# Chunked retention attention and channel mix: scores on 64-row tiles, decay moved to key and eviction, a 128x128 state for two heads, mix in blocks of 256 tokens one block behind, everything in written order

## The chip, the core and the metric

The kernel runs on one core of one Trainium2 chip. The metric is the device time of the whole program in microseconds (us). Times are medians of several executions. The traces come from one profiled execution each, whose span is some 1 to 3 us shorter than the median.

In these kernels TensorE (PE) runs the matmuls and transposes, and PEld is its weight load; VectorE (DVE) and ScalarE (ACT) run elementwise operations, those that empty TensorE's accumulators (PSUM) among them; GpSimd (POOL) runs elementwise operations between tiles in SBUF and issues the casting loads, and SyncE (SP) issues plain loads and stores. The page of the kernel before counts 1456, 1456, 214, 178 and 19 instructions on PE, PEld, DVE, ACT and POOL.

## The reference, cut to what matters

```python
# q, k, v: [B=4, H=8, S=768, D=64] float32
gamma = 1 - 2 ** (-5 - arange(H)); scale = 1 / sqrt(D)
for t in range(S):
    state = gamma * state + einsum("bhd,bhe->bhde", k[:, :, t], v[:, :, t])
    y[:, :, t] = scale * einsum("bhd,bhde->bhe", q[:, :, t], state)
x = y as [B, S, 512]
x_prev = x shifted by one token, zero first
xk = mu_k * x + (1 - mu_k) * x_prev          # token mix, for the keys
xr = mu_r * x + (1 - mu_r) * x_prev          # token mix, for the gate
out = sigmoid(xr @ w_r) * (maximum(xk @ w_k, 0) ** 2 @ w_v)   # 512 -> 1024 -> 512
```

The recurrence is worked in chunks of 128 tokens: masked scores inside a chunk, and a state of 64x64 per head carried from chunk to chunk. There are 24 chunks.

## The kernel before

The kernel before lets a scheduler interleave the attention of one batch with the mix of the batch before. These are the parts that matter. The decay is multiplied into q and k on DVE, in one operation of 1024 columns per chunk. The mix works in halves of 384 tokens, and its difference `dx` is made on POOL.

```python
# attention, per chunk (cut)
nc.vector.tensor_tensor(out=qks, in0=qk32, in1=Gqk, op=ALU.mult)       # L199: decay on q and k
... transposes of q and k by TensorE, copied out by ACT (zero-padded qptz) and DVE (kpt)
nc.tensor.matmul(pA[:, jj], lhsT=kpt[:, j, :], rhs=qptz[:, :, j, :])   # L214: 128 rows, half of them zeros
nc.vector.tensor_tensor(out=a2t[...], in0=pA, in1=causal8[...])        # L218
...
nc.scalar.copy(out=xT[:, :, col : col + C], in_=pY)                    # L238: attention output
nc.vector.tensor_tensor(out=s16g, in0=pS, in1=ghv2, op=ALU.mult)       # L256: state, 256 columns

# mix, per half of 384 tokens (cut)
nc.gpsimd.tensor_tensor(out=dx, in0=xcur, in1=xprev, op=ALU.subtract)  # L129
for fo in range(NJ):
    nc.vector.scalar_tensor_tensor(out=xk16[:, fo], in0=dx[:, fo], scalar=muk4[...], in1=xprev[:, fo], ...)  # L135
    nc.vector.scalar_tensor_tensor(out=xr16[:, fo], ...)               # L139
... keys (L148), relu and square (ACT), values (L160), gate (L166), product osb (DVE), store
```

Of the kernel before, what the change touches and what calls it, by code (L numbers as in the profile page):

```python
# [9 lines left out]
F16 = mybir.dt.float16  # L11
# [4 lines left out]
KSC = 64.0  # L16
DX_ON_POOL = True
KPT_ON_ACT = True


def _f16(x):
    return np.asarray(x, dtype=np.float32).astype(np.float16)
# [3 lines left out]
def kernel(  # L26
# [20 lines left out]
    TM = 384  # L47
    NTM = S // TM
    COLS = S + 1
    NCO = dm // P  # L50
    NFO = dff // P
    ntb = TM // P
    INV_KSC2 = 1.0 / (KSC * KSC)
# [3 lines left out]
    e3 = np.ones((1, 1, D))  # L57
    Gqk_np = np.stack(
        [(0.125 * gam[None, :, None] ** ar[:, None, None]) * e3,
         (gam[None, :, None] ** (-ar[:, None, None])) * e3], axis=1,  # L60
    )
    causal_np = (ar[None, :] >= ar[:, None]).astype(np.float64)
    causal8_np = np.broadcast_to(causal_np[:, None, :], (C, H, C)).copy()
    hp_of_p = np.arange(P) // 64
    h_pj = 2 * np.arange(NJ)[None, :] + hp_of_p[:, None]
    ghv2_np = np.broadcast_to((gam[h_pj] ** C)[:, :, None], (P, NJ, D)).copy()
    eye = np.eye(D)
    dz = np.zeros((P, 2, D))
    dz[0:64, 0] = eye
    dz[64:128, 1] = eye  # L70
    ident_np = np.eye(P)

    const_pool = ctx.enter_context(tc.tile_pool(name="consts", bufs=1))
    wpool = ctx.enter_context(tc.tile_pool(name="weights", bufs=1))
    xpool = ctx.enter_context(tc.tile_pool(name="xstage", bufs=1))
    qk_pool = ctx.enter_context(tc.tile_pool(name="qkp", bufs=3))
    v_pool = ctx.enter_context(tc.tile_pool(name="vp", bufs=2))
    awork = ctx.enter_context(tc.tile_pool(name="awork", bufs=3))
    spool = ctx.enter_context(tc.tile_pool(name="spool", bufs=3))
    mwork = ctx.enter_context(tc.tile_pool(name="mwork", bufs=2))  # L80
    psT = ctx.enter_context(tc.tile_pool(name="psT", bufs=1, space=bass.MemoryType.PSUM))
    psA = ctx.enter_context(tc.tile_pool(name="psA", bufs=1, space=bass.MemoryType.PSUM))
    psY = ctx.enter_context(tc.tile_pool(name="psY", bufs=1, space=bass.MemoryType.PSUM))
    psS = ctx.enter_context(tc.tile_pool(name="psS", bufs=1, space=bass.MemoryType.PSUM))
    psZ = ctx.enter_context(tc.tile_pool(name="psZ", bufs=1, space=bass.MemoryType.PSUM))
    psV = ctx.enter_context(tc.tile_pool(name="psV", bufs=2, space=bass.MemoryType.PSUM))
    psR = ctx.enter_context(tc.tile_pool(name="psR", bufs=1, space=bass.MemoryType.PSUM))

    c32_np = np.concatenate([Gqk_np.reshape(P, -1), ghv2_np.reshape(P, -1)], axis=1)
    c16_np = np.concatenate([ident_np.reshape(P, -1), causal8_np.reshape(P, -1)], axis=1)  # L90
    c32d = nc.inline_tensor(c32_np.astype(np.float32), name="c32")
    c16d = nc.inline_tensor(c16_np.astype(np.float16), name="c16")
    c32 = const_pool.tile(list(c32_np.shape), F32, name="c32_sb")
    c16 = const_pool.tile(list(c16_np.shape), F16, name="c16_sb")
    nc.sync.dma_start(out=c32, in_=c32d.ap())
    nc.sync.dma_start(out=c16, in_=c16d.ap())
    n0 = Gqk_np.reshape(P, -1).shape[1]
    Gqk = c32[:, 0:n0].rearrange("p (a h d) -> p a h d", a=2, h=H)
    ghv2 = c32[:, n0:].rearrange("p (j e) -> p j e", j=NJ)
    ident = c16[:, 0:P]  # L100
    causal8 = c16[:, P : P + H * C].rearrange("p (h t) -> p h t", h=H)

    xT = xpool.tile([P, NJ, B * COLS], F32, name="xT")
    for b in range(B):
        nc.vector.memset(xT[:, :, b * COLS : b * COLS + 1], 0.0)

    qptz0 = xpool.tile([P, 2, NJ, C], F16, name="qptz0")
    qptz1 = xpool.tile([P, 2, NJ, C], F16, name="qptz1")
    qptzb = [qptz0, qptz1]
    nc.vector.memset(qptz0, 0.0)  # L110
    nc.vector.memset(qptz1, 0.0)

    muk4 = const_pool.tile([P, NCO], F32, name="muk4")
    mur4 = const_pool.tile([P, NCO], F32, name="mur4")
    nc.sync.dma_start(out=muk4, in_=moe_mu_k.rearrange("(co ci) -> ci co", ci=P))
    nc.sync.dma_start(out=mur4, in_=moe_mu_r.rearrange("(co ci) -> ci co", ci=P))

    wk16 = wpool.tile([P, NCO, dff], F16, name="wk16")
    wv16 = wpool.tile([P, NFO, dm], F16, name="wv16")
    wr16 = wpool.tile([P, NCO, dm], F16, name="wr16")  # L120

    def moe_block(b):
        for half in range(NTM):
            colx = b * COLS + 1 + half * TM
            xcur = xT[:, :, colx : colx + TM]
            xprev = xT[:, :, colx - 1 : colx + TM - 1]
            dx = mwork.tile([P, NJ, TM], F32, tag="dx")
            if DX_ON_POOL:
                nc.gpsimd.tensor_tensor(out=dx, in0=xcur, in1=xprev, op=ALU.subtract)  # L129
            else:  # L130
                nc.vector.tensor_tensor(out=dx, in0=xcur, in1=xprev, op=ALU.subtract)
            xk16 = mwork.tile([P, NJ, TM], F16, tag="xk16")
            xr16 = mwork.tile([P, NJ, TM], F16, tag="xr16")
            for fo in range(NJ):
                nc.vector.scalar_tensor_tensor(  # L135
                    out=xk16[:, fo], in0=dx[:, fo], scalar=muk4[:, fo : fo + 1],
                    in1=xprev[:, fo], op0=ALU.mult, op1=ALU.add,
                )
                nc.vector.scalar_tensor_tensor(  # L139
                    out=xr16[:, fo], in0=dx[:, fo], scalar=mur4[:, fo : fo + 1],  # L140
                    in1=xprev[:, fo], op0=ALU.mult, op1=ALU.add,
                )
            krel = mwork.tile([P, NFO, TM], F32, tag="krel")
            k2 = mwork.tile([P, NFO, TM], F16, tag="k2")
            for fo8 in range(NFO):
                pZ = psZ.tile([P, TM], F32, tag="pZ")
                for co in range(NCO):
                    nc.tensor.matmul(  # L148
                        pZ, lhsT=wk16[:, co, fo8 * P : fo8 * P + P], rhs=xk16[:, co, :],
                        start=(co == 0), stop=(co == NCO - 1),  # L150
                    )
                nc.scalar.activation(out=krel[:, fo8, :], in_=pZ, func=AF.Relu, scale=KSC)  # L152
                if fo8 % 4 == 3:
                    hsl = slice(fo8 - 3, fo8 + 1)
                    nc.scalar.activation(out=k2[:, hsl], in_=krel[:, hsl], func=AF.Square)  # L155
            for tb in range(ntb):
                tsl = slice(tb * P, tb * P + P)
                pV = psV.tile([P, dm], F32, tag="pV")
                for fo8 in range(NFO):
                    nc.tensor.matmul(  # L160
                        pV, lhsT=k2[:, fo8, tsl], rhs=wv16[:, fo8, :],
                        start=(fo8 == 0), stop=(fo8 == NFO - 1),
                    )
                pR = psR.tile([P, dm], F32, tag="pR")
                for co in range(NCO):
                    nc.tensor.matmul(  # L166
                        pR, lhsT=xr16[:, co, tsl], rhs=wr16[:, co, :],
                        start=(co == 0), stop=(co == NCO - 1),
                    )
                rsb = mwork.tile([P, dm], F32, tag="rsb")  # L170
                nc.scalar.activation(out=rsb, in_=pR, func=AF.Sigmoid)  # L171
                osb = mwork.tile([P, dm], F32, tag="osb")
                nc.vector.scalar_tensor_tensor(  # L173
                    out=osb, in0=pV, scalar=INV_KSC2, in1=rsb, op0=ALU.mult, op1=ALU.mult,
                )
                s0 = half * TM + tb * P
                nc.sync.dma_start(out=out[b, s0 : s0 + P, :], in_=osb)

    for b in range(B):
        v16 = v_pool.tile([P, H, NCH, D], F16, tag="v16")  # L180
        nc.gpsimd.dma_start(
            out=v16.rearrange("t h c d -> t (h c) d"),
            in_=v[b].rearrange("h (c t) d -> t (h c) d", t=C),
        )
        if b == 0:
            nc.gpsimd.dma_start(out=wk16, in_=moe_w_k.rearrange("(co ci) f -> ci co f", ci=P))
            nc.gpsimd.dma_start(out=wv16, in_=moe_w_v.rearrange("(fo fi) e -> fi fo e", fi=P))
            nc.gpsimd.dma_start(out=wr16, in_=moe_w_r.rearrange("(co ci) e -> ci co e", ci=P))
# [100 lines left out]
```

## Time and profile before

| what | before |
|---|---|
| median of 3 runs, profiled span | 268.99 us, 266.6 us |
| busy PE, DVE, ACT, POOL | 193.7, 147.1, 110.0, 33.7 us |
| first mix matmul starts at | 55.8 us |
| columns that TensorE streams, all / by 56 us | 357,376 / 22,656 |
| time at half clock in the clock records | 44.1 us |

Half clock means that a clock record of the profile gives 0.50 as the granted share of TensorE's full clock. Read the busy time of PE as how long some matmul was in flight, not as a limit that was reached: at the full clock 357,376 columns take some 149 us (an estimate, from matmuls of 512 columns that start 216 ns apart in the trace of before, some 2.4 columns a ns).

### The profile page before, as it was taken

How to read it: one execution, taken by the hardware profiler on the slowest of the kernel's cores; microseconds unless marked ns; L12 is line 12 of the kernel's file. 1: busy time of each engine (PE TensorE's matmuls, PEld its weight loads, DVE VectorE, ACT ScalarE, POOL GpSimd, SP SyncE). 2: the span in 40 equal slices, each digit the busy share in tenths (PEclk: the TensorE clock that was granted, in tenths of full speed). 3: DMA queues.
4: the chain of work that ended last, by engine and by line, in shares of the span. 5: the costliest groups of instructions: out<-in, count | busy, mean ns of one | idle time of the engine just before them, and what ended most of it. 6: DMA issues, size and time to landing. Idle time of an engine off the chain costs nothing. (4 is left out here: it accounts for less than half of the span.)

```text
span 266.6 us, 3608 instructions
## 1 busy us (share of the span) xinstructions
PE 193.7 (73%) x1456; PEld 107.2 (40%) x1456; DVE 147.1 (55%) x214; ACT 110.0 (41%) x178; POOL 33.7 (13%) x19
## 2 busy tenths in 40 slices
PE   0020356683999997683999994859999987598883
PEld 0010234461454555451544553634554464233431
DVE  1022146889955256989644179799451479912103
ACT  1010122233375753431564662244747653255640
POOL 8200000407000001215000004040000040400000
PEclk9999999978699998786899997597999999889999
DMA  5999999736954426509907045300320110000203
GB/s 152 170 185 197 189 157 191 162 81 41 211 126 135 122 57 185 115 2 102 173 0 199 1 140 138 80 2 0 79 100 20 48 73 0 0 4 31 87 0 118
DMA packets 81472, 25.82 MB, mean 97 GB/s; under 512 B 76080, under 2 KB 77616, under 8 KB 81456
## 3 DMA queue, kind: packets, MB, share of 16 engines
q1 hardware_dynamic: 54720, 19.83, 31.3%
q0 software_dynamic: 26736, 5.77, 23.8%
q8 instruction: 11, 0.18, 0.3%
q14 instruction: 5, 0.04, 0.0%
HBM read 25.07 MB, written 6.29 MB: 118 GB/s over the span
## 5 line engine op out<-in xcount | busy, mean ns | idle before, releaser
L148 PE MATMUL pZ<-xk,wk 128*128 128x384 f16 x256 | 59.2, 347 | 1.9 <-ACT krel L152 1.1
L199 DVE TENSOR_TENSOR qks<-qk,c_sb 128x1024 f16<-128x1024 f32 x24 | 34.9, 1468 | 45.3 <-DMA qk<-in_k_dram 26.3
L160 PE MATMUL pV<-wv,k 128*128 128x512 f16 x192 | 48.0, 380 | 3.5 <-ACT k L155 3.3
L152 ACT ACTIVATE krel<-pZ 128x384 f32<-128x384 f32 x64 | 31.2, 488 | 44.7 <-PE pZ L148 44.6
L218 DVE TENSOR_TENSOR a2t<-pA,c_sb 128x512 f16<-128x512 f32 x48 | 33.0, 688 | 27.6 <-PE pA L214 27.3
L166 PE MATMUL pR<-wr,xr 128*128 128x512 f16 x96 | 33.3, 425 | 15.6 <-DVE xr L139 14.8
L129 POOL TENSOR_TENSOR dx<-xT 128x1536 f32<-128x1536 f32 x8 | 22.0, 2749 | 175.0 <-ACT xT L238 156.3
L148 PEld LDWEIGHTS <-wk 128*128 128x128 f16 x256 | 26.2, 103 | 28.4 <-issue 14.0
L173 DVE SCALAR_TENSOR_TENSOR osb<-pV,rsb 128x512 f32<-128x512 f32 x24 | 16.4, 686 | 31.8 <-PE pV L160 13.7
L238 ACT COPY xT<-pY 128x512 f32<-128x512 f32 x24 | 14.1, 586 | 47.1 <-PE pY L233 39.7
L139 DVE SCALAR_TENSOR_TENSOR xr<-dx,mur,xT 128x384 f16<-128x384 f32 x32 | 33.4, 1044 | 0.0
L228 PE MATMUL pY<-a2t,v 128*64 128x128 f16 x192 | 25.7, 251 | 9.6 <-DVE a2t L218 9.0
L206 ACT COPY qptz<-pT 64x512 f16<-64x512 f16 x24 | 13.8, 576 | 35.4 <-PE pT L203 35.4
L202 PE MATMUL pT<-c_sb,qks 128*128 128x128 f16 x96 | 17.6, 251 | 14.3 <-DVE qks L199 14.3
L160 PEld LDWEIGHTS <-k 128*128 128x128 f16 x192 | 17.3, 98 | 23.5 <-ACT k L155 6.1
L243 PE MATMUL pS<-v,qks 128*64 128x64 f16 x192 | 9.5, 218 | 22.3 <-DVE qks L199 19.8
L155 ACT ACTIVATE k<-krel 128x1536 f16<-128x1536 f32 x16 | 23.7, 1484 | 0.5
L214 PE MATMUL pA<-qptz,kpt 128*128 128x256 f16 x96 | 22.2, 318 | 1.8 <-DVE a2t L218 1.8
L171 ACT ACTIVATE rsb<-pR 128x512 f32<-128x512 f32 x24 | 14.3, 595 | 21.5 <-PE pR L166 13.7
L233 PE MATMUL pY<-qptz,s16g 128*64 128x128 f16 x160 | 22.2, 247 | 0.0
L228 PEld LDWEIGHTS <-v 128*64 128x64 f16 x192 | 17.3, 122 | 12.2 <-issue 11.5
L166 PEld LDWEIGHTS <-xr 128*128 128x128 f16 x96 | 10.0, 104 | 28.4 <-DVE xr L139 19.6
(25 smaller groups left out, 152.0 us busy)
## 6 DMA issues: line engine op xcount, KB each, us to landing
qk<-in_q_dram SPq DMA_DIRECT2D x24, 256.0 KB, 3.8
qk<-in_k_dram SPq DMA_DIRECT2D x24, 256.0 KB, 4.1
out_dram<-osb SPq DMA_DIRECT2D x24, 256.0 KB, 2.1
v<-in_v_dram POOLq DMA_DIRECT2D x4, 768.0 KB, 12.8
wk<-in_moe_w_k_dram POOLq DMA_DIRECT2D x1, 1024.0 KB, 19.9
wv<-in_moe_w_v_dram POOLq DMA_DIRECT2D x1, 1024.0 KB, 25.8
c_sb<-c SPq DMA_DIRECT2D x1, 640.0 KB, 3.6
wr<-in_moe_w_r_dram POOLq DMA_DIRECT2D x1, 512.0 KB, 28.4
```

What stands on the lines that cost most here:

```text
L129: nc.gpsimd.tensor_tensor(out=dx, in0=xcur, in1=xprev, op=ALU.subtract)
L139: nc.vector.scalar_tensor_tensor(out=xr16[:, fo], in0=dx[:, fo], scalar=mur4[:, fo : fo + 1], in1=xprev[:, fo], op0=ALU.mult, op1=ALU.add,)
L148: nc.tensor.matmul(pZ, lhsT=wk16[:, co, fo8 * P : fo8 * P + P], rhs=xk16[:, co, :], start=(co == 0), stop=(co == NCO - 1),)
L152: nc.scalar.activation(out=krel[:, fo8, :], in_=pZ, func=AF.Relu, scale=KSC)
L155: nc.scalar.activation(out=k2[:, hsl], in_=krel[:, hsl], func=AF.Square)
L160: nc.tensor.matmul(pV, lhsT=k2[:, fo8, tsl], rhs=wv16[:, fo8, :], start=(fo8 == 0), stop=(fo8 == NFO - 1),)
L166: nc.tensor.matmul(pR, lhsT=xr16[:, co, tsl], rhs=wr16[:, co, :], start=(co == 0), stop=(co == NCO - 1),)
L199: nc.vector.tensor_tensor(out=qks, in0=qk32, in1=Gqk, op=ALU.mult)
L214: nc.tensor.matmul(pA[:, jj], lhsT=kpt[:, j, :], rhs=qptz[:, :, j, :], start=(jj == 0), stop=(jj == 1),)
L218: nc.vector.tensor_tensor(out=a2t[:, 4 * tt : 4 * tt + 4, :], in0=pA, in1=causal8[:, 0:4, :], op=ALU.mult,)
L228: nc.tensor.matmul(o, lhsT=v16[:, h, c, :], rhs=a2t[:, h, :], start=first, stop=(last and c == 0), skip_group_check=(hp == 1),)
L233: nc.tensor.matmul(o, lhsT=s16g_prev[:, j, :], rhs=qptz[:, hp, j, :], start=False, stop=last, skip_group_check=(hp == 1),)
```

## The change

The intent is to feed TensorE without gaps. Its parts are:

- the queries are loaded as 16-bit numbers by a casting load and not scaled at all; the decay of the query is multiplied in at the eviction of the attention output, which moves from ACT to DVE;
- the decay of the key is multiplied by POOL (`kscale`);
- scores use 64 rows per head (128*128 with half of the rows zero before), so no zero padding is needed, and the heads of a pair go to two PSUM tiles;
- the state of two heads is one 128x128 tile, of which the eviction keeps the two diagonal blocks;
- the mix works in 256-token blocks, the gate and values of a block stand one block behind its keys, and the written order is kept on every engine;
- for the start, the constants are smaller, v is loaded chunk by chunk and no longer a batch at a time, and the weights are loaded behind the first two chunks.

```diff
-            nc.vector.tensor_tensor(out=qks, in0=qk32, in1=Gqk, op=ALU.mult)
+        nc.gpsimd.tensor_tensor(
+            out=KS[c], in0=K32[c], in1=gk[:, :, None].to_broadcast([P, H, D]), op=ALU.mult
+        )
...
+        for j in range(NJ):
+            for hp in range(2):
+                r = slice(hp * D, hp * D + D)
+                nc.tensor.matmul(
+                    pA[hp][:, j, :], lhsT=QKT[c][r, 1, j, :], rhs=QKT[c][r, 0, j, :],
...
-            nc.scalar.copy(out=xT[:, :, col : col + C], in_=pY)
+        nc.vector.tensor_tensor(out=xT[b][:, :, col : col + C], in0=pY, in1=gy, op=ALU.mult)
...
+    for m in range(NBLK + 1):
+        a = 2 * (m + 1)
+        p = m - 1
+        z = m < NBLK
+        if p > 0:
+            store(p - 1, 1)
+        maybe(load, a + 2)
+        maybe(load, a + 3)
+        maybe(scores, a)
+        maybe(state, a)
+        if z:
+            keys(m, 0)
... (scores and state of a + 1, keys 1, retained a, keys 2, retained a + 1, keys 3)
+        maybe(shift, m + 1, NBLK)
+        maybe(ahead, a + 2)
+        if p >= 0:
+            gate(p, 0)
+        maybe(ahead, a + 3)
+        if p >= 0:
+            gate(p, 1)
+            values(p, 0)
+            store(p, 0)
+            values(p, 1)
```

Here `shift` is dx on POOL and the eight mix operations on DVE, `ahead` is the key scaling on POOL and the transposes on TensorE, and `retained` is the attention output with its eviction. I call one pass of the loop a turn and measure it from the start of one dx to the start of the next. I call a mix operation held when it lasts over 0.8 us where others of its size take 0.47.

## The prediction

> **What bounds the kernel now.** I read the page's busy table and slices first, then the stretches of 20 us, then the sums of waits, then DVE's and POOL's order of time around the two kinds of hole. The page:
>
> ```profile
> PE 193.7 (73%) x1456; PEld 107.2 (40%) x1456; DVE 147.1 (55%) x214; ACT 110.0 (41%) x178; POOL 33.7 (13%) x19
> ...
> PE   0020356683999997683999994859999987598883
> ...
> PEclk9999999978699998786899997597999999889999
> DMA  5999999736954426509907045300320110000203
> ```
>
> PE is the busiest, but it is neither full nor evenly filled: the first six slices (40 us) are half full at most while DMA stands at 9, and about every 57 us (once a batch) there is a dip in which the granted clock falls too. In stretches (columns: PE, PEld, DVE, ACT, POOL busy us, then clock, DMA share, GB/s):
>
> ```profile
> 0.00:20.00 20.00, 1.47 (x16) 1.20 (x16) 2.77 (x8) 2.44 (x3) 7.19 (x9) 1.00 1.28 169
> 20.00:40.00 20.00, 6.71 (x60) 4.60 (x60) 5.96 (x10) 2.91 (x5) 0.00 (x0) 1.00 1.38 181
> ...
> 60.00:80.00 20.00, 14.73 (x89) 7.39 (x89) 17.20 (x20) 9.81 (x16) 5.03 (x2) 0.83 1.00 126
> 80.00:100.00 20.00, 19.95 (x143) 10.22 (x141) 8.99 (x14) 12.38 (x20) 0.00 (x0) 1.00 0.38 105
> ```
>
> From 0 to 40 us DMA is over 100% (packets overlap) and PE has 8 us of work. From 60 to 80 DVE is full and PE waits; from 80 to 100 PE is full. The sums of waits name the causes, DMA at the start and DVE's token mix at the dips:
>
> ```profile
> DVE qks L199 <- DMA qk<-in_k_dram: 26.3, 5, 11.0
> ...
> PE pR L166 <- DVE xr L139: 14.8, 4, 4.7
> ...
> PE pT L202 <- DVE qks L199: 14.3, 1, 14.3
> ```
>
> Why a mix operation takes so long, DVE and then POOL in order of time:
>
> ```profile
> 118.63 0.61 DVE L135 SCALAR_TENSOR_TENSOR xk<-dx,muk,xT 128x384 f16<-128x384 f32 x1
> 119.16 5.13 DVE L139 SCALAR_TENSOR_TENSOR xr<-dx,mur,xT 128x384 f16<-128x384 f32 x1
> 124.21 0.41 DVE L208 COPY kpt<-pT 128x512 f16<-128x512 f16 x1
> ```
>
> ```profile
> 118.83 2.25 POOL L181 DMA_DIRECT2D v<-in_v_dram  x1 [10.21 <-DVE xr L139]
> 121.10 2.76 POOL L129 TENSOR_TENSOR dx<-xT 128x1536 f32<-128x1536 f32 x1
> ```
>
> The mix of 0.61 us lasts 5.13 us: it ends 0.43 us after POOL's dx ends (123.86). At 61.94 the same happens (5.05 us), and at 177.28 and 226.81 with dx alone (3.11 us each). DVE work from PSUM beside dx is not held: an a2t at 217.70 takes its 0.69 us while dx runs from 216.93 to 219.68.
>
> [...] at 119.16 the wait began under the v issue; whether that alone blocks, or the dx queued behind it, this trace cannot tell. [...] in its clock records of 3.4 us the half grants follow windows that matmul columns filled less than about 0.4. [...] The kernel before has no row tiles, so nothing here shows the gain; I count none.
>
> **The change, part by part.**
>
> *TensorE.* Columns streamed, before: 98,304 (pZ) + 98,304 (pV) + 49,152 (pR) + 24,576 (pA) + 45,056 (pY) + 24,576 (pT) + 17,408 (pS) = 357,376. After: the same three mix parts 245,760 + transposes 24,576 + scores 192 x 128 = 24,576 + state 96 x 128 + 20 x 512 = 22,528 + retained 192 x 128 + 80 x 128 = 34,816, in all 352,256. Starts lie 56 ns apart for 128 columns, 162 for 384, 216 for 512, some 2.4 columns a ns; so 147 us instead of 149. The matmuls are not where it gains. One full block of 256 tokens is 29,696 columns, 12.4 us.
>
> *DVE.* Gone: qks (34.9 us busy), kpt (9.9). Added: the pY eviction with its decay (24 x 512 columns, from ACT), and the state eviction doubles to 512. PSUM operations of 512 columns start 0.60 us apart and of 256 columns 0.33 apart, so 1.05 ns a column; a mix operation of 384 is 0.53 apart, hence of 256 about 0.40. After: (48 a2t + 24 state + 24 xT + 24 osb) x 0.60 = 72, plus 96 mix operations x 0.40 = 38: 110 us against 147. A block is 10 x 0.60 + 8 x 0.40 = 9.2 us.
>
> *ACT* per block: 4 x (0.60 relu + 0.63 square), 2 transposed copies of 1024 at about 1.0, 2 sigmoids at 0.60: 8.1 us. No bound.
>
> *POOL* gets work: the key scaling, and q and v as casting loads, 48 instead of 4. dx is 2.75 us for 1536 columns, 1.79 ns each: 1.83 us for a block's 1024, and 0.92 for a key scaling of 512. An issue of 1,024 pieces (wv) took 0.89. A block: 4 x 0.88 + 1.83 + 2 x 0.92 = 7.2 us.
>
> *DMA.* Cast packets took 31.7 ns, plain ones of 256 bytes 20.4 (means over the trace). After: 49,152 x 31.7/16 = 97 us of all 16 engines, k 31, output 17, weights 15: 160 us against 147. Spread over 220 us it does not bind.
>
> *The start.* Constants shrink from 928 KB to some 330, and weights no longer overtake whole batches of v. But POOL's order has ten loads and both late weights before the first key scaling, and the wv issue waits[...] for v of chunk 1 to land. Chunks 0 and 1 are 4 x 2.03 + 2 x 1.3 + about 1 = 11.6 us of engine time; at the 1.33 of the first 40 us, 8.7 us after about 4, plus landing: 14. Key scaling ends near 16 and 17, transposes, copy and scores take it to 19, DVE's eight evictions (8 x 0.60) to 24.
>
> *The chain that I think sets a block.* Count from the end of DVE's last xT eviction. POOL runs dx until 2.0 (with 0.1 for signals), and only then, in its written order, the next key scaling, until 2.95. PE finished its last keys group at about 0.2 and its next instructions are the transposes of that key: it waits 2.8 us. Then transposes, two gates and two values to 9.05, scores, state and first keys to 10.8, and the rest (second scores and state behind their evictions, keys 1 and 2, both retained) to 14.9; xT at 15.65. So a block costs 15.65 us where the columns alone would cost 12.4. A hole of 2.8 us leaves a 3.4 us window under 0.4 filled in about 60% of positions ((3.4 + 2.8 - 2 x 2.05)/3.4); a half-clock window then costs 1.7: 1.05 on average, so 16.7 us.
>
> *On DVE beside it.* The eight mix operations come right behind dx, when POOL starts two key scalings and then, with nothing to wait for, four issues. [...] If only the scalings hold it, the mix is done by 7.1 and PE's chain of 16.7 decides. I take 17.0.
>
> *Sum.* First xT 24; block 0, without output work, 15; nine blocks x 17.0 = 153; the last attention block 14; then keys left over 0.2, three rounds of gates and values 3 x 5.2, keys 3.5, last product 0.7, store 2.1: 22. That is 228 us of span. The runs are some 2 us above the profiled span (268.99 against 266.6)[...]. I predict 226.
>
> **Rivals.** (1) All of POOL holds DVE: 17.8 to 18.5 a block, 237 to 243. For it, the two 5 us mix operations; against it, both had a dx queued behind the issue. (2) The kernel reaches PE's own bound because signals or POOL are faster than reckoned or row tiles pair well: 12.4 to 13.5 a block, 185 to 198. For it, the full stretch at 80 to 100; against it, the written order puts key scaling behind dx, and all eight dx took 2.74 to 2.76 us. (3) DMA binds because casting packets are dearer and twice as many: 160/1.33 = 120 us, so only the start could feel it, 5 to 8 us more. (4) No gain, because PE's columns are the same: it would need 16 us of PE waiting more than I find, per block 19.9; about the case of (1) with cold windows everywhere.
>
> **Range and chances.** The gain is the start (first a2t work before at 27.5 and the first mix matmul at 55.8, now near 30) and dips shared out among blocks. From (2) softened and (1): 206 to 243. Even (1) with a late start stays 8% under 269, so faster 0.96, same 0.03, slower 0.01.
>
> **What would show it.** Right: PE idle once per block before the transposes, released by POOL's key scaling, 2 to 3 us; mix operations of over 1 us whose ends follow POOL's; half-clock windows repeated; PE busy over 80%; twelve beats of 16 to 18 us. Wrong: a beat under 14 us (then the key scaling is not late), or PE held mostly by DVE evictions or by loads of q (then the chain is another).

What a reader needs to follow the rest:

- *The sum.* It came to 228 us of span, and 2 us for the runs above the span make 230. From this a term for packed 64-row tiles was taken off. What the trace of the changed kernel shows of such tiles is that the two scores of a pair start 3 to 4 ns apart and pairs some 56 ns.
- *DVE beside it.* The first of two cases was the estimate, from the times of dx, key scaling and issue given above: if all of POOL's work held the mix, the mix would start at 2.0 + 2 x 0.92 + 4 x 0.88, some 7.3 us, and xT would end at about 17.8. The second case is the one that stands, and 17.0 was taken between 16.7 and 17.8.
- *The clock.* The 60% of positions and the 1.7 us for each are the estimate from the clock records of before, where half clock lasts 3.4 us or a multiple of it (but for the last, 3.1). The windows of 3.4 us in front of one at half clock were filled to between 0.05 and 0.45 there, counted in columns started, at 2.4 a ns; but the windows that start before 50.5 us, filled to between 0.00 and 0.49, were followed by none (the first half grant is at 53.9), so 0.4 is a reading of these records and no more.
- *ACT and signals.* The times taken for ACT and the 0.1 us for signals have no source in the text. The changed kernel has 0.60 us for relu, 0.63 for square, 1.01 for a transposed copy and 0.60 for a sigmoid; its dx starts 0.08 to 0.15 us after xT ends, and the mix 0.03 to 0.04 us after dx.

## The result, and the profile after

The changed kernel takes 227.2 us (226.44 to 228.75, 4 runs) against 269.56 us of the kernel before beside it (267.73 to 270.2, 4 runs). The ratio is 0.8457, with a 95% interval of 0.8407 to 0.8508. Ratios are the mean time of one kernel's fast runs over that of the other's fast runs of the same rounds, so they are not quite the ratio of the medians.

The page of the changed kernel, in the same rows as before (busy times; then 40 slices in tenths):

```profile
PE 169.7 (75%) x1444; PEld 106.8 (47%) x1444; DVE 132.4 (59%) x220; ACT 98.3 (44%) x146; POOL 94.5 (42%) x92
...
PE   0128495877869977986868977986878986999993
...
PEclk9999999699996996999996996999996996999999
```

The empty start is shorter (the fourth slice, of 5.6 us, is the first at 8; before it was the ninth, of 6.7), the wide dips are gone, and in their place stands a small one in each turn. The clock row shows the small ones too: a 6 in about two turns of three.

The sums of waits name the new bound (who waited for whom: us in all, times, longest):

```profile
PE pT L117 <- POOL ks L108: 34.5, 12, 7.1
DVE xk L188 <- POOL dx L183: 24.7, 12, 2.1
...
PE pS L141 <- DVE sbd L150: 7.3, 12, 0.8
```

None of the waits of the kernel before that the prediction shows is among them. TensorE waits twelve times for POOL's scaled key: 7.1 us once before the loop, 3.2 and 0.6 us in the first two turns, and then 2.63 us in each of nine. One turn in order of time, TensorE first (the last two lines are the same place in an earlier turn):

```profile
82.80 0.39 PE L115 MATMUL pT<-c_sb,q 128*128 128x128 f16 x4
85.81 0.61 PE L117 MATMUL pT<-c_sb,ks 128*128 128x128 f16 x4 [2.63 <-POOL ks L108]
86.21 1.91 PE L213 MATMUL pR<-wr,xr 128*128 128x512 f16 x4
...
52.20 0.40 PE L117 MATMUL pT<-c_sb,ks 128*128 128x128 f16 x4 [2.63 <-POOL ks L108]
52.44 1.03 PE L213 MATMUL pR<-wr,xr 128*128 128x512 f16 x4
```

The hole is 2.63 us in both. Behind it, the four gate matmuls took 1.91 us at 86.21 and 1.03 us at 52.44: the first ran at half clock (granted 0.50 from 86.21 to 88.20, 1.00 from 52 to 54). POOL and then DVE in the same turn:

```profile
82.86 1.89 POOL L183 TENSOR_TENSOR dx<-xT 128x1024 f32<-128x1024 f32 x1 [10.14 <-DVE xT L174]
84.72 2.22 POOL L108 TENSOR_TENSOR ks<-k,csm_sb 128x512 f16<-128x512 f32 x2
86.89 0.94 POOL L102 DMA_DIRECT2D q<-in_q_dram  x1
```

```profile
84.79 3.23 DVE L188 SCALAR_TENSOR_TENSOR xk<-dx,muk,xT 128x256 f16<-128x256 f32 x4 [2.07 <-POOL dx L183]
87.94 1.67 DVE L188 SCALAR_TENSOR_TENSOR xr<-dx,mur,xT 128x256 f16<-128x256 f32 x4
```

POOL sits idle for 10 us until the last xT is evicted, makes dx, and only then scales the key that TensorE is waiting for. The four xk operations take 3.23 us where the four xr take 1.67: the two xk that lie beside the two key scalings take 1.25 and 1.26 us instead of 0.47, and end 0.29 us after them. The xr run at their plain speed, 0.47 us each, although POOL issues loads beside them.

The eleven turns last 12.99, 13.05, 15.87, 17.74, 17.41, 15.86, 17.75, 17.50, 15.86, 17.75 and 17.54 us.

**Where the 41 us of span come from.** By 56 us the kernel before had streamed 22,656 columns and the changed one 52,736. At the later rate of the kernel before, (357,376 - 22,656) columns in (266.6 - 56) us, 1.59 a ns, that lead is worth 19 us. After 56 us the changed kernel runs at 1.77 columns a ns: its last 299,520 columns take 169.6 us instead of 188.5, another 19. The 5,120 columns fewer are worth 3.

### The profile page after: what moved, and what is told of

It is laid out like the page before. It is cut to its first block, busy times and chain, and to the rows that moved or that the text cites. A ratio compares the mean times of both kernels' runs of the same rounds, so it can differ in the third digit from the quotient of the medians.

```text
span 225.6 us, 3597 instructions
## 1 busy us (share of the span) xinstructions
PE 169.7 (75%) x1444; PEld 106.8 (47%) x1444; DVE 132.4 (59%) x220; ACT 98.3 (44%) x146; POOL 94.5 (42%) x92
## 3 DMA queue, kind: packets, MB, share of 16 engines
q0 software_dynamic: 52544, 8.92, 50.5%
## 4 chain that ended last, share of the span: by engine, by line
PE 53%; DVE 16%; issue 11%; POOL 11%; DMA 8%; POOLq 0%; DVEq 0%
PE pV L223 18%; PE pR L213 12%; PE pZ L200 10%; DMA v<-in_v_dram 8%; DVE a2t L132 5%; POOL ks L108 5%; PE pT L117 3%; PE pY L168 3%; DVE osb L232 3%; DVE xT L174 3%; DVE sbd L150 3%; POOL q L102 2%; PE pY L162 2%; PE pS L141 2%; POOL v L104 2%
## 5 line engine op out<-in xcount | busy, mean ns | idle before, releaser
L183 POOL TENSOR_TENSOR dx<-xT 128x1024 f32<-128x1024 f32 x12 | 22.7, 1888 | 106.1 <-DVE xT L174 106.1
L205 ACT ACTIVATE kr<-pZ 128x512 f32<-128x512 f32 x48 | 28.6, 596 | 65.1 <-PE pZ L200 64.9
L188 DVE SCALAR_TENSOR_TENSOR xk<-dx,muk,xT 128x256 f16<-128x256 f32 x48 | 37.1, 832 | 24.7 <-POOL dx L183 24.7
L200 PE MATMUL pZ<-xk,wk 128*128 128x256 f16 x384 | 51.0, 279 | 0.0
L119 ACT COPY qkT<-pT 128x1024 f16<-128x1024 f16 x24 | 24.3, 1013 | 44.2 <-PE pT L117 44.0
L117 PE MATMUL pT<-c_sb,ks 128*128 128x128 f16 x96 | 12.5, 270 | 34.7 <-POOL ks L108 34.5
L206 ACT ACTIVATE k<-kr 128x512 f16<-128x512 f32 x48 | 30.2, 630 | 1.5
L108 POOL TENSOR_TENSOR ks<-k,csm_sb 128x512 f16<-128x512 f32 x24 | 26.4, 1119 | 0.1
L174 DVE TENSOR_TENSOR xT<-pY,gy_sb 128x512 f32<-128x512 f32 x24 | 16.6, 691 | 12.9 <-PE pY L168 12.5
L102 POOL DMA_DIRECT2D q<-in_q_dram x24 | 22.3, 928 | 0.8 <-POOLq L325 0.8
L104 POOL DMA_DIRECT2D v<-in_v_dram x24 | 21.6, 898 | 0.4 <-DMA v<-in_v_dram 0.4
L188 DVE SCALAR_TENSOR_TENSOR xr<-dx,mur,xT 128x256 f16<-128x256 f32 x48 | 19.9, 473 | 0.0
## 6 DMA issues: line engine op xcount, KB each, us to landing
wk<-in_moe_w_k_dram POOLq DMA_DIRECT2D x2, 512.0 KB, 12.7
```

Of the source, the lines that this page charges most:

```text
L102: nc.gpsimd.dma_start(out=Q16[c], in_=q[b, :, t, :].rearrange("h t d -> t h d"))
L104: nc.gpsimd.dma_start(out=V16[c], in_=v[b, :, t, :].rearrange("h t d -> t h d"))
L108: nc.gpsimd.tensor_tensor(out=KS[c], in0=K32[c], in1=gk[:, :, None].to_broadcast([P, H, D]), op=ALU.mult)
L117: nc.tensor.transpose(pT[:, 1, j, :], KS[c][:, 2 * j : 2 * j + 2, :], ident)
L119: nc.scalar.copy(out=QKT[c], in_=pT)
L188: nc.vector.scalar_tensor_tensor(out=dst[:, j], in0=dx[:, j], scalar=mu[:, j : j + 1], in1=xprev[:, j], op0=ALU.mult, op1=ALU.add,)
```

## The experiments

Twelve kernels ran, all with correct results. Edits are against the changed kernel unless another is named.

### Key scaling in front of dx (e1_key_first)

```diff
+        maybe(kscale, a + 2)
+        maybe(kscale, a + 3)
         maybe(shift, m + 1, NBLK)
-        maybe(ahead, a + 2)
+        maybe(transposes, a + 2)
```

(the same for chunk a + 3 and, before the loop, for chunks 2 and 3)

> Edit: in POOL's order the two key scalings stand before the difference dx instead of behind it; nothing else moves. Theory (the chain retained, xT, dx, key scaling, transposes sets the block): PE no longer waits about 2.7 us before the key transposes, the half-clock windows go with the hole[...]; a block falls from 17.0 us to about 13, the span from 225.6 to 186 to 194 us. Rival A (DVE's evictions set the block): DVE has 9.2 us of work in 17.0, so under it the block stays above 16 and the time above 215. Rival B (casting loads set it): time unchanged, 222 to 230.

Measured: 203.46 us, ratio 0.757 (0.7523 to 0.7618). The hole is gone, and nothing but the order of POOL's instructions was changed: the wait was the bound, and rivals A and B fall. (From the third turn on, the hold of the mix goes with the hole; e3 keeps it.) But the time lies 9 us above the expected range. Two things are behind that. The first is in POOL's order of time:

```profile
81.40 2.04 POOL L108 TENSOR_TENSOR ks<-k,csm_sb 128x512 f16<-128x512 f32 x2 [6.13 <-DMA k<-in_k_dram]
83.41 1.88 POOL L183 TENSOR_TENSOR dx<-xT 128x1024 f32<-128x1024 f32 x1
```

The key scaling now waits for its load, which stands on SP's queue behind a store that waits for DVE (the stores are issued at 75.67, the loads of k at 76.71). The last xT ended at 82.40, so dx starts 1.0 us late. Turns from the third on last 13.4 to 13.9 us (the very last 12.7). The second is that the first two turns became longer, 16.01 and 16.49 us instead of 12.99 and 13.05. DVE in the first of them:

```profile
25.49 3.24 DVE L188 SCALAR_TENSOR_TENSOR xk<-dx,muk,xT 128x256 f16<-128x256 f32 x4 [2.01 <-POOL dx L183]
28.66 3.26 DVE L188 SCALAR_TENSOR_TENSOR xr<-dx,mur,xT 128x256 f16<-128x256 f32 x4
```

In both turns four operations are held instead of two. The two turns cost 6.5 us; without that the time would have been at 197. But the hold is not alone in them: the clock records hold 13.7 us at half clock there (the changed kernel: 3.4), and TensorE waits 2.84 us for a load of q. The shares are not separated. I come back to this with e7 to e10.

### Work in the hole (e2_filler)

```diff
+        for j in range(32 if c >= 6 and c % 2 == 0 else 0):
+            nc.tensor.transpose(pT[:, 0, j % NJ, :], Q16[c][:, 2 * (j % NJ) : 2 * (j % NJ) + 2, :], ident)
         for j in range(NJ):
             nc.tensor.transpose(pT[:, 1, j, :], KS[c][:, 2 * j : 2 * j + 2, :], ident)
```

> Edit: from chunk 6 on, 32 more transposes of q (which is there already) are put into the hole in front of the first key transposes of each block, about 1.8 us of PE work that computes nothing new. Theory: the hole stays, but no 3.4 us window is nearly empty, so the half grants after it go; the nine blocks that lasted 15.9, 17.7 and 17.5 us in turn all last 15.9: about 10 us less, 213 to 219. Rival A (the clock costs nothing, because PE has slack before the next eviction): 225 to 228, unchanged. Rival B (PE's own work sets the block): 1.8 us more in each of 9 blocks, 242.

Measured: 220.2 us, ratio 0.8181 (0.8137 to 0.8226). Adding 1.8 us of useless matmuls to a turn made the kernel 7 us faster. TensorE in one turn:

```profile
83.41 1.95 PE L117 MATMUL pT<-c_sb,q 128*128 128x128 f16 x32
86.20 0.40 PE L119 MATMUL pT<-c_sb,ks 128*128 128x128 f16 x4 [0.84 <-POOL ks L108]
86.44 1.03 PE L215 MATMUL pR<-wr,xr 128*128 128x512 f16 x4
```

The gate behind the hole takes 1.03 us in every turn; turns last 15.86 to 16.08 us; the clock records hold 4.3 us at half clock instead of 26.4. The time is 1 us above the range, for the second turn lasts 14.61 us instead of 13.05. It holds no filler yet, and no load explains it: TensorE waits 1.15 us for q there, 1.81 in the changed kernel. What differs is that its half-clock window lies later (from 45.5 instead of 40.8) and that TensorE waits longer for DVE (0.95 and 0.81 us, against 0.41); why is open. Rival A, slack that hides the clock, and rival B fall.

### TensorE's order changed, POOL's and DVE's kept (e3_pe_order)

```diff
+        maybe(kscale, a + 2)
+        maybe(kscale, a + 3)
         if p >= 0:
             gate(p, 0)
-        maybe(ahead, a + 3)
-        if p >= 0:
             gate(p, 1)
             values(p, 0)
             store(p, 0)
+        maybe(transposes, a + 2)
+        maybe(transposes, a + 3)
+        if p >= 0:
             values(p, 1)
```

> Edit: POOL's order is as in the changed kernel (dx, then the key scalings), but in PE's order both gates and the first values stand before the transposes, so PE has 3.5 us of work while it would wait[...]. Theory: the hole goes, the block is then bound by DVE behind the held mix, about 14.5 us; time 200 to 207, between the kernel with the scalings first and the changed one. Rival [...]: 220 to 228. [...]

(The rival was that the hold of the mix, and not TensorE's wait, sets the block.)

Measured: 202.42 us, ratio 0.7538 (0.7496 to 0.7579), in the range. POOL still makes dx before the keys, and DVE is still held (22 of its 96 mix operations, as in the changed kernel), yet turns from the third on last 14.03 to 14.25 us. (ACT's order follows TensorE's: its copies of the transposes now stand behind the sigmoids.) The transposes of the key no longer wait:

```profile
79.22 1.89 PE L223 MATMUL pV<-wv,k 128*128 128x512 f16 x8
...
81.17 0.39 PE L117 MATMUL pT<-c_sb,ks 128*128 128x128 f16 x4
```

So the hold of the mix alone is not what sets the 17 us. It equals e1 in time but not in build: e1's later turns are shorter by 0.6 us and its first two longer by 6.5.

### The start (e4_key_first_start)

```diff
 (against e1)
     nc.gpsimd.dma_start(out=wk16[:, :, f], in_=wks[:, :, f])
+    kscale(0)
+    kscale(1)
     load(2)
```

> Edit: as the kernel with key scalings first, and at the start the first two key scalings are moved in front of eight later loads' issues in POOL's order. Theory: the first scores no longer wait behind the issue that needs v of chunk 1 (scaling at 14.3 us); xT of chunks 0 and 1 comes 4 to 6 us earlier, bounded by v of chunk 1 landing at about 13; so 4 to 6 us under the run with scalings first alone, 181 to 189. Rival (the start is bound by the loads of wk and q): the same as that run within 1 us.

Measured: 198.1 us, ratio 0.7361 (0.732 to 0.7402). That is 5.4 us under e1, as expected of the difference; the absolute range was set on e1's expected time and missed with it. The first key scaling starts at 6.63 us instead of 14.31 and the first dx at 20.16 instead of 23.55.

### No neighbouring row pairs (e5_no_pairs)

```diff
-        for j in range(NJ):
-            for hp in range(2):
+        for hp in range(2):
+            for j in range(NJ):
                 r = slice(hp * D, hp * D + D)
```

> Edit: the score matmuls of a chunk go through all four pairs of one 64-row half and then through the other, so that no two neighbours sit on different halves of the array (in the changed kernel the two of a pair start 3 ns apart and pairs 56 ns apart). Eight scores then take about 0.45 us instead of 0.22, 0.45 us of PE more per block. Theory: in the changed kernel PE waits 0.4 to 0.8 us per block for the state eviction just behind the scores, and DVE is busy with the output products when the first scores come, so the added time falls into waits: 0 to 2 us more, 226 to 229. Rival (row pairing is a main part of the gain): 5 us or more, above 232.

Measured: 228.14 us, ratio 0.8499 (0.8463 to 0.8536), which is not to be told from the changed kernel (0.8457). But the run did not do what it was made for. The scores of one chunk, in the changed kernel and then in e5:

```profile
58.16 0.40 PE L126 MATMUL pA<-qkT 64*128 64x128 f16 x8
...
59.78 0.41 PE L126 MATMUL pA<-qkT 64*128 64x128 f16 x8
```

One by one, the eight start at 0, 4, 67, 70, 123, 126, 179 and 182 ns in the changed kernel and at 0, 13, 66, 79, 122, 135, 178 and 191 ns in e5: still two by two, and nowhere near the 0.45 us that was expected. So the equal times say nothing of what row pairs are worth, and neither the theory of this run nor its rival is tested. Why the new order still runs in pairs is open.

An estimate from the changed kernel's steps says that it cannot be much. From a keys matmul to the first score it is 0.205 us and from one keys matmul to the next 0.109; from the last score to the state it is 0.148 where nothing waits, against 0.056 between state matmuls. So going from the 128-row matmuls to the 64-row ones and back costs some 0.19 us a chunk. Eight scores one after the other, 56 ns each as the 128-row matmuls of 128 columns start apart, would take 0.45 us instead of the 0.22 of four pairs, so pairing would save 0.22, of which little is left.

### Gate and values in the same turn (e6_same_block)

```diff
-    for m in range(NBLK + 1):
+    for m in range(NBLK):
         a = 2 * (m + 1)
-        p = m - 1
+        p = m
```

> Edit: gates and values of a block are worked in the same turn as its keys, not one block behind. Theory: the turn's length is set by the chain through dx and the key scaling, and gates and values fill PE behind the transposes in either case; the lag costs one round of gates and values (5.2 us) in the tail and gives it back in the first turn, which had none: 224 to 229. Rival (the lag is what keeps PE fed): PE waits 1.2 us per block for the squares, 12 us or more, above 236.

Measured: 226.38 us, ratio 0.8433 (0.8386 to 0.8481). The lag of one block, which is part of the change's title, brings nothing measurable in this kernel, whose turns the wait for the key sets; in the faster ones below it was not tried. From the second on, turns are 16.1 to 17.6 us: the second is longer (16.09 instead of 13.05), and the part behind the last dx shorter (17.9 us instead of 23.1).

### Loads before the store, two key buffers (e7_best)

```diff
 (against e4)
+        maybe(load_k, a + 2)
+        maybe(load_k, a + 3)
         if p > 0:
             store(p - 1, 1)
-        maybe(load, a + 2)
-        maybe(load, a + 3)
+        maybe(load_qv, a + 2)
+        maybe(load_qv, a + 3)
...
-        KS[c] = att.tile([P, H, D], F16, name="ks16")      # 4 buffers
+        KS[c] = ksp.tile([P, H, D], F16, name="ks16")      # 2 buffers
```

> Edit: as the run with key scalings first and an early start, and in addition the k loads of a turn stand on SP's queue in front of the store that waits for DVE, and the scaled keys have two buffers instead of four, so that a key scaling waits for PE's state two chunks back and cannot be ready while the mix runs. Theory: in the run before, a turn of 13.7 us was the loop mix, output product, store issue, k loads (5.2 us to landing), two key scalings, dx; with the loads out of it the turn is dx 1.9, mix 3.2, outputs 1.2, six evictions 3.6, wait and xT 2.6: about 12.6; nine turns shorter by 1.05 and the first two no longer 15: 183 to 188. Rival (PE or DMA binds at 13.5): 195 to 199, unchanged.

Measured: 193.28 us, ratio 0.7191 (0.7159 to 0.7223). It is faster than e4, but it lies above the expected range and under the rival's: from the third on, turns last 13.1 to 13.4 us and not 12.6. No mix operation is held, and after the first turn dx follows xT within 0.3 us; so that loop was opened. The first turn is still 15.75 us with nothing held: TensorE waits 5.15 and 2.65 us in it for loads of q, while the DMA row of its page stands at 9. So the hold is not what makes the first turn long here. In the later turns what came next was TensorE itself: the output product waits 0.55 us for its values, and behind the scores stands the one wait that is left:

```profile
98.39 0.38 PE L150 MATMUL pS<-sbd,c_sb 128*128 128x512 f16 x1 [0.78 <-DVE sbd L159]
```

### Four key buffers again (e8_keys_early)

```diff
 (against e7)
-    ksp = pool("ksp", 2)
+    ksp = pool("ksp", 4)
```

> Edit: e7 with four buffers for the scaled keys again and nothing else, so a key scaling is ready to run behind the four issues, while DVE mixes. Theory: as in the first two turns of the run with key scalings first (mix operations held twice, 3.2 us in all, turns of 16.0 and 16.5 us), every turn becomes about 15.5 to 16: 205 to 218. Rival (those two turns were slow from the start's loads and half clock[...]): equal to e7 within 2 us.

Measured: 195.57 us, ratio 0.7269 (0.7224 to 0.7314). The run did not test what it was made for: from the third turn on the key's load came late, and nothing was ready behind the issues. Only its second turn, where k was there, had four held operations and lasted 16.18 us against 13.62 in e7; TensorE's waits for q in it are alike in the two (3.4 and 3.3 us). From the third turn on, turns are 13.1 to 13.5 us, so the earlier loads bring e7's later turns without the two buffers. So I loaded k earlier still.

### Keys ready behind the issues, and its control (e9_k_ahead_keys_early, e10_k_ahead)

```diff
 (both against e7; e9 has 4 key buffers, e10 has 2)
-        maybe(load_k, a + 2)
-        maybe(load_k, a + 3)
+        for c in (4, 5, 6, 7) if m == 0 else (a + 4, a + 5):
+            maybe(load_k, c)
```

> Edit: as e10 (k loaded one turn further ahead), with four buffers for the scaled keys instead of two, so that both key scalings of a turn can run as soon as POOL has issued the four loads that stand in front of them. In e8 this was meant but k came too late from its third turn on; its second turn, where k was there, had four held mix operations and lasted 16.18 us against 13.62 in e7. Theory: an elementwise POOL instruction that is ready behind issues holds DVE's two-SBUF-input operations while the issues run; 4 of 8 mix operations held in each turn, 3.2 us of DVE, turns near 15.7 to 16.3: 212 to 224. Rival (only the start did that): no held operations, within 2 us of e10.

> Edit: e7 with k loaded one turn further ahead (seven buffers). Theory: in e7 the key scalings still wait for k, until just before dx, but dx comes within 0.3 us of xT, so nothing is lost; a turn stays 13.1 to 13.3 and the time within 2 us of e7: 190 to 195. If k's landing were still in the loop, 186 or less.

Measured: e9 228.88 us, ratio 0.8536 (0.8494 to 0.8577); e10 195.86 us, ratio 0.7302 (0.7273 to 0.7331). The two differ in one number, the count of key buffers, and more buffers cost 33 us. (e10 missed its range by 0.9 us and is 2.6 above e7: its second turn lasts 17.08 us with nothing held, for TensorE waits 6.28 us for q in it.) POOL and then DVE of e9 in one turn:

```profile
105.89 0.96 POOL L108 DMA_DIRECT2D q<-in_q_dram  x1
...
109.46 2.30 POOL L118 TENSOR_TENSOR ks<-k,csm_sb 128x512 f16<-128x512 f32 x2
```

```profile
105.98 3.30 DVE L198 SCALAR_TENSOR_TENSOR xk<-dx,muk,xT 128x256 f16<-128x256 f32 x4 [2.07 <-POOL dx L193]
109.21 3.23 DVE L198 SCALAR_TENSOR_TENSOR xr<-dx,mur,xT 128x256 f16<-128x256 f32 x4
```

Two of the four xk of 105.98 to 109.28 are held (at 106.38 and 107.63) while POOL's records show nothing but issues of loads (105.89 to 109.48); the key scalings are recorded from 109.46 on, and then two of the xr are held as well. In e10, beside the same four issues (80.88 to 84.46), DVE runs through:

```profile
80.97 1.67 DVE L198 SCALAR_TENSOR_TENSOR xk<-dx,muk,xT 128x256 f16<-128x256 f32 x4 [2.01 <-POOL dx L193]
82.56 1.67 DVE L198 SCALAR_TENSOR_TENSOR xr<-dx,mur,xT 128x256 f16<-128x256 f32 x4
```

In e9 35 of 96 mix operations (each reads dx and xT, both in SBUF) are held, in e10 none. The time is above the expected range: all turns but the first and the last are 16.9 to 17.5 us, because TensorE's longer waits bring half clock, 38.0 us of it (e7: 8.5).

### State before scores (e11_state_first)

```diff
 (against e7; the same for a + 1)
-        maybe(scores, a)
         maybe(state, a)
+        maybe(scores, a)
```

> Edit: e7 with a chunk's state matmuls in front of its scores instead of behind. Theory: a turn of e7 (13.2 us) has 0.56 to 0.78 us in which PE waits for DVE's eviction of the first chunk's state, which comes behind two score evictions; with the state first it is evicted earlier and the wait goes: turns of 12.5, 184 to 188. Rival (DVE's own order binds): unchanged, 191 to 194.

Measured: 190.33 us, ratio 0.7095 (0.7068 to 0.7123), the fastest kernel. TensorE's waits for the state's eviction fall from 6.3 us in ten to 2.0 us in seven, but the turns from the third on only to between 12.8 and 13.1 us (the last 12.0), not to 12.5, so the time misses the range by 2 us. TensorE is close to what it can do there: the columns of a full turn are 12.4 us of work (an estimate: 29,696 at 2.4 a ns, from the 216 ns between matmuls of 512 columns). The page:

```profile
PE 161.0 (86%) x1444; PEld 103.8 (55%) x1444; DVE 113.3 (60%) x220; ACT 95.7 (51%) x146; POOL 92.8 (49%) x92
...
PE   0256139679999999999999999999999999999991
```

What is left is the start, the first nine slices. Its largest wait of TensorE is for loads of q (21.2 us in six waits, the longest 7.5); in the changed kernel that wait is 9.9 us in three.

### The kernel before with dx on DVE (b1_dx_on_dve)

```diff
 (against the kernel before)
-DX_ON_POOL = True
+DX_ON_POOL = False
```

> Edit: the kernel before, with the difference dx on DVE instead of POOL (its own switch), eight of 1536 columns, about 1.7 us each, 14 us more DVE work. Theory: the held operations of before (8, some 2.5 us each, and 2.3 more where a v issue stands in front) vanish, about 24 us of DVE waiting for 14 of DVE work, but three of the four first halves lie where DVE has little else; and DVE's dips stay, for its mix work is what fills them: 258 to 268, a change of -4% to 0. Rival [...]: 245 or less.

Measured: 244.59 us, ratio 0.9107 (0.9062 to 0.9151). My theory of this run failed, and the time is that of its rival: that the held operations made the dips of before. The clock row of its page and DVE around one of its dx:

```profile
PEclk9999999589999999569999999999999999999999
```

```profile
60.47 0.61 DVE L139 SCALAR_TENSOR_TENSOR xr<-dx,mur,xT 128x384 f16<-128x384 f32 x1
61.00 1.75 DVE L131 TENSOR_TENSOR dx<-xT 128x1536 f32<-128x1536 f32 x1
62.66 1.22 DVE L199 TENSOR_TENSOR qks<-qk,c_sb 128x1024 f16<-128x1024 f32 x1
```

DVE makes dx in 1.75 us and goes on; in the kernel before it lost 4.4 us at that place (5.05 for a mix operation of 0.61). Over the whole trace of before, seven DVE operations were held for 20.0 us in all (their durations less 0.61 for a mix operation and 1.21 for qks). Against that stand eight dx, 13 us (1.66 us each from start to start). What I had left out is the clock: half clock falls from 44.1 us to 18.3, and 25.8 us at half clock are 13 us of TensorE's work (an estimate: half of them, as the four gate matmuls took 1.91 us at half clock and 1.03 at the full one in the changed kernel). The two together, 7 and 13, make up most of the 24 us; that sum is an account, not a separate measurement. Nor is dx all that moved: this kernel leaves the order to the scheduler, and TensorE's order differs from that of before from the 190th matmul or so on, DVE's and ACT's too. Which part of the 24 us is the new order was not tried. After 56 us this kernel streams (357,376 - 24,704) columns in (244.0 - 56) us, 1.77 a ns, the same rate as the changed kernel.

## Why the prediction was right, point by point

- **The block's chain.** The prediction had TensorE wait 2.8 us per block for the key scaling behind dx, and 15.65 us for a block at full clock. The trace has 2.63 and 15.86. e1 and e3 show by two different edits that this wait was the bound: moving the scaling on POOL, or moving other work in front of the wait on TensorE, took 24 and 25 us. The chain inside fits too: in the turn from 49.26 the scores behind the values start 9.05 us after xT, as predicted.
- **The clock.** The prediction had a half-clock window in about 60% of blocks at 1.7 us each. Six of the nine long turns have one (17.41 to 17.75 us against 15.86), 1.55 to 1.9 us each. e2 shows it: with the hole filled, all nine are at 15.86 to 16.08.
- **DVE beside it.** Between the two cases of the prediction, all of POOL holding the mix or only the scalings, the trace decides for the scalings: the mix ends 6.9 us after xT (7.1 predicted), and xr beside issues run in 0.47 us. The question that the prediction left open, whether an issue alone blocks, has a sharper answer in the runs: beside issues alone none of the 96 mix operations of e10 was held, and with four key buffers, so that an elementwise instruction can be ready behind the issues, 35 of 96 were (e9). Rival 1, that all of POOL's work holds DVE, is thus wrong as it was put, for issues alone held nothing in e10; what is right in it is what e9 shows, 17.2 us a turn.
- **The sum.** It was 24 + 15 + 153 + 14 + 22 = 228; the trace has 23.1 to the end of the first two chunks' xT, 179.3 for the eleven turns and 23.2 behind. Inside it, terms were wrong in opposite ways: the first turn lasts 12.99 and not 15; the second 13.05 and not 17, for the first gates and values come a turn later than I counted; and the last attention turn 17.54 and not 14, for the loads that it lacks seem not to have been in the chain. The eight turns between have a mean of 16.97.
- **Luck in the number.** That 226 lies within 1.2 us of 227.2 is in part luck. The errors of the turns nearly cancel, and 228 of span and 2 for the runs would have been 230; the 4 us taken off for packed 64-row tiles are shown by nothing. The mechanism of the long turns does not rest on this. One sum does not come out: rival 4 needs 39 us more than the predicted 228 to reach 266.6, not 16.
- **Its signs.** Most came true. PE busy was to be over 80% and is 75%; the beats were to be twelve of 16 to 18 us, and of eleven nine are 15.9 to 17.8. A beat under 14 was named as a sign of being wrong: the first two are 13, in which no gates and values stand.
- **POOL's terms** were sized a little low: a key scaling takes 1.02 us alone and 1.12 in the loop, not 0.92; dx 1.89, not 1.83; an issue 0.9, not 0.88.
- **The start.** Scalings were to end near 16 and 17, the trace has 15.35 and 16.35; the wait for v of chunk 1 is there (the wv issue starts at 13.34).
- **What was off in the reading of before.** The prediction saw the hold in before (5.13 us for a mix operation of 0.61), but it names DVE's token mix as the cause of the dips, and the theory of b1 gave the hold 4% at most. b1 shows that taking dx off POOL, with the order that the scheduler then makes, is worth 24 of the 269 us without anything else of the change.
- **Rivals 2 and 3.** TensorE's own bound was out of reach of this order, but not of the parts: e11 runs turns of 13 us. Casting loads did not bind after the start: DMA stayed below full in every stretch after 66 us (share 0.68 to 0.73 from 66 to 174). In the second turn TensorE does wait 1.8 us for q, and in the faster kernels such waits in the first two turns are longer (e7, e10).

What in the change made the gain is settled only in part. By the account above half of it is the start, half the later rate, and the later rate is what b1 reaches with dx alone. That the lag of a block brings nothing here is shown (e6); what the row pairs bring is not, for e5 did not undo them. Which of the start's edits (smaller constants, loads chunk by chunk, weights behind them) brings how much was not tried.

## What to carry to other kernels

When two engines both stand on the path of every turn, look at the order inside the slower one: two key scalings moved in front of a subtraction were worth more than half of what the whole rewrite had brought. Count a hole in TensorE twice, once as itself (2.63 us here) and once as the half clock that may follow (1.55 to 1.9 us more in six turns of nine). And look at what GpSimd works on elementwise, or has ready behind its load issues, while VectorE mixes: beside a key scaling a mix operation took 1.25 us instead of 0.47, and 35 of 96 were held in e9 where in e10, with fewer key buffers, none was; fewer buffers can be the way out.

## What the runs show of the hardware

- Mix operations, which read dx and xT in SBUF, took 1.25 us instead of 0.47 beside a key scaling (22 of 96 in the changed kernel), where an a2t out of PSUM beside dx took its 0.69 (217.70 in the kernel before). The hold began before the record of the GpSimd instruction did in e9: mix operations were held up to 3.1 us before the key scaling's recorded start (from 106.38 on, recorded at 109.46), with only load issues in between. In e10, where the key scaling has two buffers instead of four, none was held. What holds them in that time no run here shows.
- In the changed kernel a step to or from a group of scores took 0.09 to 0.10 us more than one without a change (0.205 against 0.109, 0.148 against 0.056), which by the estimate under e5 is nearly all of the 0.22 us that pairing saves on eight 128-column matmuls.
- Half clock followed windows of 3.4 us that were filled to a third (0.34 at 37.38 and 81.76 in the changed kernel). Counting the columns started in them, at 2.4 a ns, the windows before half clock were filled to 0.16 to 0.34 in the changed kernel (the one behind its last matmul to 0.00), and two filled to 0.44 and 0.45 were not followed by it; in the kernel before, two filled to 0.44 and 0.45 were, and one filled to 0.44 was not. At the start, until 53.9 us in the kernel before and 40.8 in the changed one, no half clock is recorded, though some windows there were filled to 0.00. Of nine turns with a hole of 2.63 us, six had half clock behind it.
